# Twenty instead of nineteen score tiles on VectorE in 25 of 64 attention groups, and four follow-up steps moved

## The chip, the cores and the metric

The kernel runs on one core of one Trainium2 chip. The metric is the device time in microseconds of one execution; the number given for a kernel is the median of several executions. A profiled execution comes with a trace of every instruction on the engines: TensorE (PE, its weight loads PEld), VectorE (DVE), ScalarE (ACT), GpSimd (POOL) and SyncE (SP).

## The reference

Two spectral layers and two attention layers alternate, each on a layer norm of the running array x (2048 rows, 512 columns, bf16), each added back to x. The change touches only the attention:

```python
def _B_ref(x, wq, wk, wv, wo):
    B, S, D = x.shape
    H = 32
    Dh = D // H
    q = (x @ wq).reshape(B, S, H, Dh).transpose(0, 2, 1, 3)
    k = x @ wk
    v = x @ wv
    scores = jnp.einsum("bhqd,bkd->bhqk", q, k) * (Dh ** -0.5)
    p = _softmax(scores, axis=-1)
    o = jnp.einsum("bhqk,bkd->bhqd", p, v)
    return o.transpose(0, 2, 1, 3).reshape(B, S, H * Dh) @ wo
...
x = x + _A_ref(_layernorm(x, axis=-1), A_w_r, A_w_i)
x = x + _B_ref(_layernorm(x, axis=-1), B_wq, B_wk, B_wv, B_wo)
x = x + _A_ref(_layernorm(x, axis=-1), A_w_r, A_w_i)
x = x + _B_ref(_layernorm(x, axis=-1), B_wq, B_wk, B_wv, B_wo)
```

There are 32 heads of 16 columns, and one set of keys and values for all of them. So per attention layer there are 32 x 2048 x 2048 exponentials.

## The kernel before

**Groups and tiles.** The kernel has two pairs of (spectral layer, attention layer). `Attention.run` (L560) does one attention layer as 32 groups: 4 blocks of 512 queries times 8 sets of 4 heads. A group has 64 score tiles: 16 blocks of 128 keys times 4 heads; a tile is 128 keys by 512 queries. For every tile TensorE makes the scores in PSUM (`score`, L681), some engine makes the exponential in SBUF, and TensorE multiplies it by the values and a column of ones into the group's sum `pv` (L803).

**Two ways to an exponential.** ScalarE takes 45 of the 64 tiles of a group, 3 and 2 at a time in turn (`OPW`), with its exponential function (`act_step`, L790: `e<-sc`). One such ScalarE instruction is one **step**; a group has 18 steps. VectorE takes the other 19 (`DPOS`, three batches of 6, 7 and 6 tiles). For such a tile it makes one linear map of the scores into 16-bit integers, whose bits read as bf16 are a rough power of two (`dv_pass`, L824: `t_new<-dv`). Three further images of the tile, shifted by fixed amounts, are added with weights to smooth the error: two by VectorE for a whole batch at once (`image_step`, L839: `s_new<-t_new`, 128x3072 for 6 tiles, 128x3584 for 7), one by GpSimd tile by tile (L843: `pool_new<-t_new`). So a VectorE tile costs TensorE one score matmul and four value matmuls, where a ScalarE tile costs one and one.

**Order of a step.** The loop at the end of `run` goes through the steps. In step n it issues, in this order: the scores and the exponential of ScalarE's step (`act_step`), the scores for VectorE's tiles of the step (`dv_score`), what a piece of the step before left for VectorE (`pending`), the turning of a finished group (`evict`, L706), `dv_pass`, what was put off to this step (`todo`), the batch images (`image_step`), what was put off for GpSimd (`todo_pool`), the value matmuls (`pv_step`) and at last a piece. All engines work through their own queue in this order.

Counted from the first step of a group (step 0): batch b is scored in the six steps before step 6b, two tiles in the first of the six where it has seven, else one a step; its two VectorE images are in steps 6b and 6b+3 (`IMG`), and its GpSimd images in steps 6b to 6b+5. In step 3 the group before is turned (L706). Its reciprocals (L707) follow one step later, and GpSimd's scaling (`normalise`, L739, or L717 for the last 8 groups of a layer) three steps after the turn.

**GpSimd's pace.** `pace` makes GpSimd's images and its scaling wait for the VectorE image issued last before them. Nothing makes a VectorE image wait for GpSimd.

**Pieces.** `QSTEP` = 7: in step 7 TensorE projects the queries of the next group (`piece("q")`, L485); VectorE scales them out of PSUM in step 8 (`qcast`, L491) and clears the sign bits of a part of the rows (`qabs`, L495, the "mask of the bound") `QABS` = 1 step after the piece. `OSTEP` = 13: in 12 groups of a layer (9 to 12, 17 to 20, 25 to 28) TensorE projects 128 of the finished outputs (`piece("o")`, L754) in step 13, and VectorE adds the old rows of x in the step after (`residual`, L759). A piece takes one of the two PSUM tiles `dv0`, `dv1`, in which VectorE's scores stand, until VectorE has read it.

In the first layer the new rows get their statistics in groups 13 to 16, 21 to 24 and at the end (L152, L153). In the last layer finished rows are stored.

Of the kernel before, what the change touches and what calls it, by code (L numbers as in the profile page):

```python
# [472 lines left out]
class Attention:  # L473
# [85 lines left out]

    def run(self, row_done, work, psums, final):  # L560
        nc, tc, tabs, x_sb, KT, small = self.nc, self.tc, self.tabs, self.x_sb, self.KT, self.small
# [24 lines left out]
        NG = NQB * HG  # L586
        ops = []
# [13 lines left out]
        for g in range(NG):  # L601
            for b, pos in enumerate(DPOS):
# [4 lines left out]
                steps = [base - BSTEPS + k for k in range(BSTEPS) for _ in range(1 + (len(pos) > BSTEPS and k in TWICE[b]))]  # L607
# [9 lines left out]
        LAG, NBT = 2, max(len(pos) for pos in DPOS)  # L617
        evict_at = {s1[g] + LAG + 1: g for g in range(NG)}
# [22 lines left out]
        for g in range(NG - 1):  # L641
            place(s0[g] + QSTEP, "q", g + 1)
        for qb in range(NQB - 1):
            for i in range(4):
                place(s0[HG * (qb + 1) + 1 + i] + OSTEP, "o", 4 * qb + i)

# [8 lines left out]
        for n in range(NS + LAG + 2):  # L655
            queue += due.get(n, [])
            lst = pv_list[n] = []
            if n in evict_at:
                assert not any(u[0] == evict_at[n] for u in queue)
                continue  # L660
            g = evict_at.get(n + 1)
            rounds = 0 if n in piece_at else ROUNDS[n % 2]
            while queue:
                rnd = full_round(queue if g is None or not any(u[0] == g for u in queue) else [u for u in queue if u[0] == g])
                must = g is not None and any(u[0] == g for u in queue)
                if not must and (rounds <= 0 or len(rnd) < 4 and len(queue) < HOLD):
# [29 lines left out]
        def evict(g):  # L696
# [9 lines left out]
            nc.vector.transpose(out=o.rearrange("p c j -> p (c j)"), in_=ps)  # L706
            later(1, lambda: nc.vector.reciprocal(out=den, in_=o[:, :, DH]))  # L707
            later_pool(3, lambda: normalise(g, o, den))

# [24 lines left out]
        def normalise(g, o, den):  # L734
# [13 lines left out]
            if g % 2:  # L748
                later(3, lambda: turned_back(g))

# [6 lines left out]
        def residual(k, ps):  # L757
            r, t = (k % 4, k // 4)
            nc.vector.tensor_tensor(out=x_sb[:, r, t, :], in0=ps, in1=x_sb[:, r, t, :], op=ALU.add)  # L759
            if t == NQB - 2:  # L760
                n = s0[NG - 3 + r // 2] + (4, 14)[r % 2]
            else:
                n = s0[HG * (t + 1) + 5 + r] + STAT
            later(max(2, n - now[0]), lambda: finish(r, t))
# [41 lines left out]

        held, bank = [None], [0]

# [18 lines left out]
        def image_step(n):  # L827
            if n in d_phase:
                g, b, k, tiles = d_phase[n]
                src, nt = tb[(g, b)].bitcast(I16), len(tiles)  # L830
                if k == 0:
                    pool_new = work.tile([P, NBT, 512], I16, tag="SP", bufs=2)
                    sb[(g, b, 3)] = pool_new
                if k in IMG:
                    i = 1 + IMG.index(k)
                    s_new = work.tile([P, NBT, 512], I16, tag="S", bufs=3)
# [28 lines left out]
        for n in range(NS + LAG + 2):  # L865
            now[0] = n
            act_step(n)
            dv = dv_score(n)
            for fn in pending:
                fn()  # L870
# [53 lines left out]
def full_kernel(ctx, tc, A_x, A_w_r, A_w_i, B_x, B_wq, B_wk, B_wv, B_wo, out, n_pairs=2):  # L924
    nc = tc.nc
# [134 lines left out]
    for pair in range(n_pairs):  # L1060
# [35 lines left out]
        with ExitStack() as ap:  # L1096
            work = ap.enter_context(tc.tile_pool(name=f"workB{pair}", bufs=2, side="right", reuse_waits="tile"))
            psums = [ap.enter_context(tc.tile_pool(name=f"{n}{pair}", bufs=1, space=PSUM, reuse_waits="tile")) for n in ("psc", "psd", "psp")]
            last = att.run(row_done, work, psums, final)
            if final:  # L1100
# [48 lines left out]
```

## Time and profile before

| | |
|---|---|
| median of 3 runs | 1523.18 us (1522.98 to 1523.98) |
| the profiled execution | 1522.62 us, its span 1520.8 us, granted TensorE clock 0.994 |
| steady group without old rows (5 groups, 174.48 to 276.34 us) | 101.86 us, 20.37 us each |
| first attention layer, ScalarE's 579 steps | begin at 106.9 us, the last at 765.0 us |
| second attention layer, ScalarE's 579 steps | begin at 854.5 us, the last at 1511.5 us |

The profile's page gives the busy time of each engine, then the chain of work that ended last, then groups of instructions by line. The windows view gives the busy time of each engine in a stretch, with the count of instructions. In the timeline, instructions of one kind in a row stand as one line with their count; a bracket shows how long the engine sat idle before, and what it waited for. Durations overlap a little: an engine starts the next instruction before the last one has fully ended, so the distance from start to start is the better price of an instruction in a busy queue.

### The profile page before, as it was taken

To read this page: it belongs to the slowest core of one execution; us is meant where nothing else is said; L and a number is where in the kernel's file an instruction comes from. 1 tells how busy PE (TensorE), PEld (TensorE's weight loads), DVE (VectorE), ACT (ScalarE), POOL (GpSimd) and SP (SyncE) were. 2 spreads that over 40 slices of the span, in tenths; PEclk is the share of its full clock that TensorE was granted. 3 is DMA by queue.
4 is the path that set the end of the run, shared out by engine and by line. 5 is a ranking of instruction groups with operands and counts; after the bars stand their busy time and mean duration, and the time that the engine had idled before them with its cause. 6 is when DMAs were issued, how large, how long until landed. Compare 5 with 4: busy or idle time off the path is not lost.

```text
span 1520.8 us, 33089 instructions
## 1 busy us (share of the span) xinstructions
PE 1337.1 (88%) x13186; PEld 427.5 (28%) x13186; DVE 1421.6 (93%) x2267; ACT 1427.3 (94%) x1349; POOL 780.1 (51%) x1310
## 2 busy tenths in 40 slices
PE   5988888899889988999899788889998899889987
PEld 2532222222222222222235222222222222222222
DVE  7888999999999999999989899999999999999996
ACT  4669999999999999999965899999999999999998
POOL 1005555555566555655600155555656555665555
PEclk9999999999999999999999899999999999999999
DMA  8120000100000000100010200000000000010000
GB/s 291 22 56 2 2 1 2 15 2 1 2 16 2 1 1 2 15 2 1 2 47 14 43 1 2 2 1 19 5 2 4 19 5 5 4 19 5 5 5 18
DMA packets 40655, 25.15 MB, mean 17 GB/s; under 512 B 31796, under 2 KB 37940, under 8 KB 40244
## 3 DMA queue, kind: packets, MB, share of 16 engines
q1 hardware_dynamic: 40116, 21.99, 5.8%
q8 instruction: 103, 1.69, 0.5%
q0 software_dynamic: 384, 1.05, 0.2%
q14 instruction: 52, 0.43, 0.1%
HBM read 14.64 MB, written 2.10 MB: 11 GB/s over the span
## 4 chain that ended last, share of the span: by engine, by line
ACT 51%; issue 22%; DVE 15%; PE 7%; POOL 1%; POOLq 0%; DVEq 0%; ACTq 0%
ACT e L790 49%; DVE t_new L824 7%; DVE s_new L839 4%; PE sc L681 1%; PE pv_new L803 1%; DVE st L161 1%; PE new L273 1%; PE new L443 1%; POOL pool_new L843 1%; DVE o L706 1%; PE new L311 0%; PE new L413 0%; DVE x_sb L459 0%; PE dv L681 0%; ACT X_new L188 0%
## 5 line engine op out<-in xcount | busy, mean ns | idle before, releaser
L790 ACT ACTIVATE e<-sc 128x1536 bf16<-128x1536 f32 (+1 forms) x1158 | 1312.7, 1300 | 4.2 <-PE dv L681 2.6
L843 POOL TENSOR_SCALAR pool_new<-t_new 128x512 int16<-128x512 int16 x1204 | 729.5, 629 | 701.9 <-DVE s_new L839 609.3
L824 DVE TENSOR_SCALAR t_new<-dv 128x512 uint16<-128x512 f32 x1204 | 790.1, 678 | 61.7 <-PE dv L681 54.3
L803 PE MATMUL pv_new<-e,vaug 128*32 128x512 bf16 x2892 | 583.3, 386 | 0.0
L681 PE MATMUL sc<-qt,KT 32*128 32x512 bf16 x2892 | 455.1, 384 | 123.4 <-ACT e L790 118.6
L681 PE MATMUL dv<-qt,KT 32*128 32x512 bf16 x1204 | 450.6, 384 | 18.9 <-DVE t_new L824 16.0
L803 PE MATMUL pv_new<-s_new,vaug 128*32 128x512 bf16 x2408 | 426.6, 385 | 1.9 <-DVE s_new L839 1.2
L839 DVE TENSOR_SCALAR s_new<-t_new 128x3584 int16<-128x3584 int16 (+1 forms) x380 | 403.3, 1062 | 0.1
L681 PEld LDWEIGHTS <-KT 32*128 32x128 bf16 x4096 | 157.9, 91 | 563.0 <-issue 559.7
L803 PE MATMUL pv_new<-pool_new,vaug 128*32 128x512 bf16 x1204 | 300.9, 384 | 1.4 <-POOL pool_new L843 1.4
L803 PEld LDWEIGHTS <-vaug 128*32 128x32 bf16 x7708 | 155.2, 94 | 370.4 <-issue 339.0
L803 PE MATMUL pv_new<-t_new,vaug 128*32 128x512 bf16 x1204 | 231.3, 385 | 0.1
L485 PE MATMUL ps<-xz,wq_sb 128*128 128x512 bf16 x248 | 65.2, 385 | 0.9 <-DVE t_new L824 0.8
L273 PE MATMUL new<-tab_F,xz 128*128 128x512 bf16 x192 | 46.5, 389 | 7.4 <-DVE xz L237 7.4
L491 DVE TENSOR_SCALAR qt<-ps,kq 128x512 bf16<-128x512 f32 x62 | 46.0, 742 | 1.2 <-PE ps L485 1.2
L706 DVE STREAM_TRANSPOSE o<-pv_new 128x512 f32<-128x512 f32 x62 | 43.7, 706 | 0.0
L188 ACT ACTIVATE X_new<-x_sb,ln_nb,ln_rstd 128x512 bf16<-128x512 bf16 x43 | 32.8, 804 | 8.0 <-DVE ln_nb L173 5.6
L161 DVE BATCH_NORM_STATS2 st<-x_sb 128x6 f32<-128x512 bf16 x52 | 33.5, 676 | 3.9 <-DMA x_sb<-in_A_x_dram 3.7
L168 ACT ACTIVATE ln_rstd<-ln_mv,ln_eps 128x4 f32<-128x4 f32 (+1 forms) x15 | 4.5, 297 | 30.8 <-DVE ln_mv L165 30.8
L485 PEld LDWEIGHTS <-wq_sb 128*128 128x128 bf16 x256 | 22.1, 97 | 32.2 <-issue 17.1
L739 POOL TENSOR_TENSOR block<-o,den 128x256 bf16<-128x256 f32 x48 | 29.9, 623 | 0.0
L197 ACT CAST x_new<-new 128x1024 bf16<-128x1024 f32 x14 | 14.2, 1012 | 16.4 <-PE new L311 15.1
(125 smaller groups left out, 586.0 us busy)
## 6 DMA issues: line engine op xcount, KB each, us to landing
tab_F<-const_F SPq DMA_DIRECT2D x5, 640.0 KB, 8.6
t_new<-const_IE SPq DMA_DIRECT2D x2, 1024.0 KB
x_sb<-in_A_x_dram SPq DMA_DIRECT2D x3, 512.0 KB, 7.0
rt<-in_A_w_r_dram SPq DMA_DIRECT2D x1, 1028.0 KB, 8.4
rt<-in_A_w_i_dram SPq DMA_DIRECT2D x1, 1028.0 KB, 6.6
t_new<-const_IO SPq DMA_DIRECT2D x2, 512.0 KB
woh<-in_B_wo_dram SPq DMA_DIRECT2D x16, 64.0 KB, 2.4
out_dram<-x_sb SPq DMA_DIRECT2D x8, 128.0 KB, 2.4
```

The source lines that it names most:

```text
L161: self.nc.vector.bn_stats(st, x_t[:, r, :])
L188: engine.activation(out=xn_ap, in_=x_ap, func=ACT.Identity, bias=nb, scale=rs)
L273: self.mm(ps, lhsT=z, rhs=tab, start=start and i == 0, stop=stop and i == len(mms) - 1)
L485: self.nc.tensor.matmul(ps, lhsT=self.aw["wq"][:, c, hg, :], rhs=self.xT[:, 4 * qb:4 * qb + 4, c, :], start=(c == 0), stop=(c == NC - 1))
L491: self.nc.vector.tensor_scalar(out=qt, in0=ps, scalar1=self.kq[:, 1:2], scalar2=None, op0=ALU.mult)
L681: nc.tensor.matmul(dst, lhsT=KT[hs, kc * P:(kc + 1) * P], rhs=QT[g][hs, :], start=True, stop=True)
L706: nc.vector.transpose(out=o.rearrange("p c j -> p (c j)"), in_=ps)
L790: nc.scalar.activation(out=e[:, 0:na, :], in_=sc[:, 0:na, :], func=ACT.Exp, scale=SCALE)
L803: nc.tensor.matmul(pv[g][32 * h:32 * h + 32, :], lhsT=vaug[:, max(j, 0), kc, :], rhs=rhs, start=(first_pv[(g, h)] == u), stop=(last_pv[(g, ...
L824: nc.vector.tensor_scalar(out=tb[(g, b)][:, i, :], in0=dv, scalar1=T_MUL, scalar2=T_ADD, op0=ALU.mult, op1=ALU.add)
L839: image[0] = nc.vector.tensor_scalar(out=s_new[:, lo:nt, :], in0=src[:, lo:nt, :], scalar1=PH_OFF[i], scalar2=None, op0=ALU.add)
L843: pace(nc.gpsimd.tensor_scalar(out=sb[(g, b, 3)][:, i, :], in0=src[:, i, :], scalar1=1.0, scalar2=PH_OFF[3], op0=ALU.mult, op1=ALU.add))
```

## The change

There are now two kinds of groups. Kind N is as before (6, 7, 6 tiles on VectorE). Kind A has batches of 7, 7 and 6, so 20 tiles on VectorE and 44 on ScalarE; one ScalarE instruction of three tiles, in step 16, becomes one of two, and the group still has 18 steps. `PLAN` names the kind of each of the 32 groups: in the first layer groups 1 to 7 are of kind A, in the second groups 1 to 8, 13 to 16, 21 to 24, 29 and 30, in all 25. None of these has old rows to add in it. The rest of the constants move into a table for each layer. In both layers and all groups four follow-ups move: the reciprocals come 2 steps after the turn instead of 1 (`RCP`), GpSimd's scaling 6 instead of 3 steps after it, but for the last 8 groups of a layer (`NRM`), the mask of the bound 3 steps after the piece instead of 1 (`QABS`), and the output projections with their old rows 2 steps later (`OSTEP` 15 instead of 13). `TFIRST` is empty, and the branch for `QABS` of zero isn't taken, so both do nothing.

```diff
-DPOS = ((1, 4, 8, 11, 15, 18), (21, 24, 27, 30, 33, 36, 39), (44, 47, 51, 54, 58, 61))
-SHORT = -1
-TWICE, IMG = ((0,), (0,), (0,)), (0, 3)
+DPOS = ({6: (1, 4, 8, 11, 15, 18), 7: (1, 4, 7, 10, 13, 16, 19)},
+        {7: (21, 24, 27, 30, 33, 36, 39)},
+        {6: (44, 47, 51, 54, 58, 61)})
+KINDS = {"N": (6, 7, 6), "A": (7, 7, 6)}
+LOOPS = (dict(PLAN='NAAAAAAANNNNNNNNNNNNNNNNNNNNNNNN',
+               SHORT=15, IMG=((0, 3), (0, 3), (0, 3)),
...
+               RCP=2, NRM=6, TRN=3, TFIRST=(), ROUNDS=(2, 4), QSTEP=7, QABS=3, OSTEP=15, STAT=14, HOLD=8),
+         dict(PLAN='NAAAAAAAANNNNAAAANNNNAAAANNNNAAN',
...
-ROUNDS, QSTEP, OSTEP, STAT, HOLD, QABS = (2, 4), 7, 13, 14, 8, 1
...
+        positions = lambda g: [DPOS[b][k] for b, k in enumerate(KINDS[C["PLAN"][g]])]
+        ops, begun = [], {}
         stream = [(g, p // 4, p % 4) for g in range(NG) for p in range(64)
-                  if not any(p in pos for pos in DPOS[g == 0:])]
+                  if not any(p in pos for pos in positions(g)[g == 0:])]
         while stream:
-            w = OPW[len(ops) % 2] - (len(ops) % 18 == SHORT)
+            g = stream[0][0]
+            n = len(ops) - begun.setdefault(g, len(ops))
+            tiles = sum(KINDS[C["PLAN"][g]])
+            w = OPW[len(ops) % 2] - (tiles == 20 and n == C["SHORT"] + (begun[g] + C["SHORT"]) % 2)
...
-            later(1, lambda: nc.vector.reciprocal(out=den, in_=o[:, :, DH]))
-            later_pool(3, lambda: normalise(g, o, den))
+            later(C["RCP"], lambda: nc.vector.reciprocal(out=den, in_=o[:, :, DH]))
+            later_pool(3 if g >= NG - HG else C["NRM"], lambda: normalise(g, o, den))
...
-                later(QABS, lambda: qabs(QT[k]))
+                if C["QABS"]:
+                    later(C["QABS"], lambda: qabs(QT[k]))
+                else:
+                    unsigned.append(lambda: qabs(QT[k]))
```

More of the change, by code (lines that the diff above doesn't have):

```diff
@@ L558, in ready, with run @@
         nc.vector.tensor_scalar(out=qt, in0=qt, scalar1=kq[:, 1:2], scalar2=None, op0=ALU.mult)
-    def run(self, row_done, work, psums, final):
+    def run(self, row_done, work, psums, final, pair):
+        C = LOOPS[pair]
         nc, tc, tabs, x_sb, KT, small = self.nc, self.tc, self.tabs, self.x_sb, self.KT, self.small
@@ L601, in run @@
         for g in range(NG):
-            for b, pos in enumerate(DPOS):
+            for b, pos in enumerate(positions(g)):
                 if g == 0 and b == 0:
@@ L606, in run @@
                 tiles = [(p // 4, p % 4) for p in pos]
-                steps = [base - BSTEPS + k for k in range(BSTEPS) for _ in range(1 + (len(pos) > BSTEPS and k in TWICE[b]))]
+                steps = [base - BSTEPS + k for k in C["DK"][b, len(pos)]]
                 clash = lambda pm: sum(any(u[2] == tiles[i][1] for u in ops[n]) for n, i in zip(steps, pm)) + \
@@ L665, in run @@
                 must = g is not None and any(u[0] == g for u in queue)
-                if not must and (rounds <= 0 or len(rnd) < 4 and len(queue) < HOLD):
+                if not must and (rounds <= 0 or len(rnd) < 4 and len(queue) < C["HOLD"]):
                     break
@@ L748, in normalise @@
             if g % 2:
-                later(3, lambda: turned_back(g))
+                later(C["TRN"], lambda: turned_back(g))
         def outproj(k, ps):
@@ L868, in run @@
             dv = dv_score(n)
+            if C["TFIRST"] and (n in evict_at and C["TFIRST"][1] or pending and C["TFIRST"][0]):
+                dv_pass(n, dv)
+                dv = []
             for fn in pending:
@@ L1098, in full_kernel @@
             psums = [ap.enter_context(tc.tile_pool(name=f"{n}{pair}", bufs=1, space=PSUM, reuse_waits="tile")) for n in ("psc", "psd", "psp")]
-            last = att.run(row_done, work, psums, final)
+            last = att.run(row_done, work, psums, final, pair)
             if final:
```

24 lines of the change are left out of this document (15 added, 9 removed).

## The prediction

> **What bounds the kernel now.** I read the page first, for the engines' busy times and the chain that ended last.
>
> ```profile
> span 1520.8 us, 33089 instructions
> PE 1337.1 (88%) x13186; PEld 427.5 (28%) x13186; DVE 1421.6 (93%) x2267; ACT 1427.3 (94%) x1349; POOL 780.1 (51%) x1310
> ACT 51%; issue 22%; DVE 15%; PE 7%; POOL 1%; POOLq 0%; DVEq 0%; ACTq 0%
> ```
>
> ScalarE and VectorE are both nearly full, so the average doesn't say which of them sets the pace. The stretches do: five steady groups without old rows; one group with them; the most loaded group of the first layer; the two groups before the last of the second.
>
> ```profile
> core 0: us, PE busy (x) PEld busy (x) DVE busy (x) ACT busy (x) POOL busy (x), PEclk, DMA share, GB/s
> 174.48:276.34 101.86, 89.02 (x948) 26.70 (x945) 96.35 (x147) 101.86 (x91) 59.67 (x101) 1.00 0.01 2
> 296.72:317.11 20.39, 19.02 (x196) 5.37 (x193) 19.75 (x32) 20.39 (x19) 11.92 (x21) 1.00 0.01 2
> 726.75:748.20 21.45, 18.67 (x192) 5.45 (x189) 21.12 (x35) 21.10 (x20) 14.05 (x25) 1.00 0.01 2
> 1453.30:1494.00 40.70, 35.56 (x381) 10.61 (x378) 39.07 (x60) 40.70 (x37) 25.69 (x43) 1.00 0.02 8
> ```
>
> In the steady stretch ScalarE is busy for all of 101.86 us: it sets 20.37 us a group. VectorE needs 96.35 / 5 = 19.27 and has 1.10 to spare; with old rows 0.64. In the loaded group the order is turned: VectorE 21.12 of 21.45, and ScalarE waits. So a group takes about the longer of the two sums, and when VectorE is the longer, some 0.33 us of it is still idle. I take the groups of the same stretch by form next.
>
> ```profile
> L790 ACT ACTIVATE e<-sc 128x1536 bf16<-128x1536 f32 x46 | 70.6, 1535 | 0.0
> L824 DVE TENSOR_SCALAR t_new<-dv 128x512 uint16<-128x512 f32 x96 | 63.2, 679 | 5.5 <-PE dv L681 4.7
> L790 ACT ACTIVATE e<-sc 128x1024 bf16<-128x1024 f32 x45 | 50.0, 1111 | 0.0
> L681 PE MATMUL sc<-qt,KT 32*128 32x512 bf16 x227 | 35.6, 381 | 11.6 <-ACT e L790 11.6
> L803 PE MATMUL pv_new<-pool_new,vaug 128*32 128x512 bf16 x95 | 23.2, 384 | 0.0
> L839 DVE TENSOR_SCALAR s_new<-t_new 128x3072 int16<-128x3072 int16 x20 | 19.0, 948 | 0.0
> L839 DVE TENSOR_SCALAR s_new<-t_new 128x3584 int16<-128x3584 int16 x10 | 12.8, 1284 | 0.0
> ```
>
> ScalarE never sits idle; VectorE's idle time ends with PE's scores, which wait for ScalarE. The odd number is the last: a seventh tile lengthens an image from 948 to 1284 ns, 336 for one sixth more work. The timeline of one steady group shows why.
>
> ```profile
> 255.95 0.71 DVE L706 STREAM_TRANSPOSE o<-pv_new 128x512 f32<-128x512 f32 x1
> 256.58 0.65 DVE L824 TENSOR_SCALAR t_new<-dv 128x512 uint16<-128x512 f32 x1
> ...
> 258.62 0.24 DVE L707 RECIPROCAL den<-o 128x16 f32<-128x16 f32 x1
> 258.77 1.38 DVE L824 TENSOR_SCALAR t_new<-dv 128x512 uint16<-128x512 f32 x2
> 260.07 1.08 DVE L839 TENSOR_SCALAR s_new<-t_new 128x3584 int16<-128x3584 int16 x1
> 261.07 0.68 DVE L824 TENSOR_SCALAR t_new<-dv 128x512 uint16<-128x512 f32 x1
> 261.67 0.74 DVE L491 TENSOR_SCALAR qt<-ps,kq 128x512 bf16<-128x512 f32 x1
> 262.33 0.68 DVE L824 TENSOR_SCALAR t_new<-dv 128x512 uint16<-128x512 f32 x1
> 262.92 0.35 DVE L495 TENSOR_SCALAR qt<-qt,tab_QAND 128x512 int16<-128x512 int16 x1
> 263.19 0.68 DVE L824 TENSOR_SCALAR t_new<-dv 128x512 uint16<-128x512 f32 x1
> 263.79 1.48 DVE L839 TENSOR_SCALAR s_new<-t_new 128x3584 int16<-128x3584 int16 x1
> 265.20 1.90 DVE L824 TENSOR_SCALAR t_new<-dv 128x512 uint16<-128x512 f32 x3
> 267.01 0.95 DVE L839 TENSOR_SCALAR s_new<-t_new 128x3072 int16<-128x3072 int16 x1
> 267.88 1.28 DVE L824 TENSOR_SCALAR t_new<-dv 128x512 uint16<-128x512 f32 x2
> 269.37 0.69 DVE L824 TENSOR_SCALAR t_new<-dv 128x512 uint16<-128x512 f32 x1 [0.21 <-PE dv L681]
> ...
> 273.05 1.29 DVE L824 TENSOR_SCALAR t_new<-dv 128x512 uint16<-128x512 f32 x2 [0.73 <-PE dv L681]
> ```
> ```profile
> 261.33 1.20 POOL L843 TENSOR_SCALAR pool_new<-t_new 128x512 int16<-128x512 int16 x2 [1.37 <-PE ps L485]
> 262.50 0.62 POOL L739 TENSOR_TENSOR block<-o,den 128x256 bf16<-128x256 f32 x1
> 263.09 1.25 POOL L843 TENSOR_SCALAR pool_new<-t_new 128x512 int16<-128x512 int16 x2
> 265.36 1.79 POOL L843 TENSOR_SCALAR pool_new<-t_new 128x512 int16<-128x512 int16 x3 [1.03 <-DVE s_new L839]
> ```
>
> The batch of seven has its first image (step 6, at 260.07) in 1.08 us and its second (step 9, at 263.79) in 1.48, though they are alike. GpSimd was then still at work until 263.09 + 1.25 = 264.34, so 0.55 of the second image ran beside it and cost 0.40. GpSimd was late because its scaling ("block") stood between its images.
>
> **The change part by part.** From start to start in a full VectorE queue: a tile (267.01 - 265.20) / 3 = 0.60; an image of six 0.87 (267.01 to 267.88); of seven 1.00 alone, 1.41 beside GpSimd; the query scaling 0.66, the mask 0.27, the turn 0.63, the reciprocal 0.15.
>
> *ScalarE in an A group* loses one tile of one instruction: 1535 - 1111 = 424 ns. Its pace becomes 20.37 - 0.42 = 19.95.
>
> *VectorE in an A group* gets one tile (0.60) and two images longer by 1.00 - 0.87 = 0.13: 0.86 more. That is inside the 1.10 only if nothing else is lost. The scaling's move out of the steps between the images of the seven-tile batch takes away the 0.40, but the images of batch 0 now run beside more GpSimd work. I go through the group, VectorE never waiting, time 0 at the image of step 0. GpSimd starts 0.18 after an image has ended (260.07 + 1.08 to 261.33) and takes 0.60 an operation.
>
> - Step 0's image 1.00, two tiles, the turn, a tile: the image of step 3 starts at 3.43. GpSimd's four tiles end at 1.26 + 2.40 = 3.66: 0.23 beside it, at 0.40 / 0.55 some 0.17.
> - Then 1.17, three tiles and the reciprocal: step 6 at 6.55. GpSimd's three tiles end at 4.86 + 1.79 = 6.65: 0.10 beside, 0.07.
> - Then 1.07, three tiles and the query scaling; the mask is gone from here: step 9 at 10.08. GpSimd's four tiles, without the scaling, end at 7.88 + 2.40 = 10.28: 0.20 beside, 0.15.
> - Then 1.15, four tiles (two of them the new batch's in step 12) and the mask: step 12 at 13.90. GpSimd's three tiles and now the scaling end at 11.49 + 2.40 = 13.89: none.
> - Then 0.87 and three tiles, 0.87 and four tiles: the next step 0 at 19.84, of which 0.39 is time beside GpSimd.
>
> The Trainium skill (SBUF — State Buffer, "Who interferes with whom") states that a VectorE instruction in a two-port mode and GpSimd exclude each other, and that the later one blocks until the first has finished. By that the overlaps would count in full, 0.53 instead of 0.39, and an A group would come out 0.14 longer on VectorE (at most 3.2 us over 23 groups, so up to 1519.7 where the row gives 1516.5); the one overlap quoted above cost 0.40 of 0.55, less than the rule says.
>
> The same walk over a group of before gives 19.84 - 0.86 - 0.39 + 0.41 = 19.00, where the row has 19.27: the walk may be 0.27 short. So VectorE in an A group needs 19.84 to 20.11, ScalarE 19.95, and the group takes between 19.95 and 20.11 + 0.33 = 20.44, if the idle time of the loaded group comes on top. I take 20.08, near the upper sum without that idle time, since an A group's load is even over the steps (images at 0, 3.43, 6.55, 10.08, 13.90, 16.57, against 3.3 each at ScalarE's pace), while the loaded group has extra work in a few. That is 0.29 less a group.
>
> *The last two* (groups 29, 30 of the second layer) keep the scaling 3 steps after the turn, so the 0.41 stays: 39.07 / 2 + 0.86 = 20.40 of VectorE against 20.35 before: nothing to win, up to 0.4 to lose each. I put them at 0.
>
> *TensorE* makes three matmuls more in an A group, from 3 x 0.244 = 0.73 (23.2 / 95) to 3 x 0.384 = 1.15, or less where four heads run side by side; it waits 11.6 / 5 = 2.32 a group for ScalarE, and even after the 0.42 there is room. Three short ScalarE steps now follow each other (15, 16, 17); if TensorE were late there the group would lose some tenths, which the upper end holds.
>
> *The moves in N groups* cost nothing that I can see. The contact of scaling and image goes from step 9 to step 12: after step 9's image, 1.00 + 0.60 x 3 + 0.27 = 3.07 to the next, GpSimd done at 3.66, 0.59 beside it. VectorE's sum stays, and 1.10 (0.64 with old rows) covers it; without cover it would be 0.4 a group. The mask in step 10 must be done before TensorE's scores of the next group in step 12; it lies two VectorE tiles ahead, so a wait there is 0 to 0.15, within the 0.27. The scaling of each eighth group issues four transposing DMAs on SyncE's queue, now three steps (3.4 us) later; the projection that reads them comes over a group later, and itself two steps later. GpSimd queues three tiles of images ahead of the scaling, and nothing else waits for that. The added old rows move from step 14 to 16, where VectorE has its idle time (0.73 at 273.05); gain or loss is about 0.02 (20.39 against 20.37) in each of 24 groups, put at 0. The reciprocal moves one step and its reader three.
>
> The sum: 23 x 0.29 = 6.7 us. From the profiled execution's 1522.62 that gives 1515.9; the median of before lies 0.56 above that execution, so **1516.5 us**.
>
> **The rivals.** *ScalarE's pace is reached in full:* VectorE keeps up. 25 x 0.42 = 10.5, so 1512.7. For it speaks that the walk's 19.84 is below 19.95; against, that no slack is left.
>
> *VectorE takes over, with idle time:* 20.3 to 20.44 a group, a gain of 1.6 to a loss of 1.6: 1521.6 to 1524.8, no change. For it speaks the loaded group's 0.33.
>
> *GpSimd's lateness spreads:* an A group has four seven-tile images. If each catches GpSimd at work as step 9's did, VectorE needs 19.45 + 4 x 0.41 = 21.09, and 23 x 0.72 = 16.6 make it 1539.8, slower. It decides from 0.65 us of contact cost in a cycle (20.37 - 19.45 - 0.27); my walk has 0.39. Against it: a contact makes the next image later, which gives GpSimd time, so contacts don't add up freely.
>
> *The move doesn't do what it says:* if GpSimd's scaling still ran before step 9's image, VectorE would be at 20.25 to 20.5: no change again.
>
> **How the numbers follow.** This kernel's measurement tells 0.2%, 3.05 us, from no change: faster is below 1520.1, slower above 1526.2. My forecast has 0.50, the full ScalarE pace 0.21; both are faster: 0.71. Idle VectorE and the unmoved scaling have 0.17 as no change. The spread of contacts, at part or full price, has 0.12 as slower. The range runs from a microsecond under ScalarE's full pace, for the few uneven groups that may even out, 1511.5, to the upper end of no slack, 1524.8; it leaves out the slow rival and a little below, some 0.15.
>
> **What would show it.** In A groups, ScalarE's 44 tiles with VectorE at 20.0 busy and about 0.1 idle; seven-tile images at 1.08 to 1.25 and none at 1.48 in the first layer's groups 1 to 7; the 1.4 us images in N groups now six-tile ones at step 12; N groups unchanged at 20.37 to 20.39. Wrong would be: A groups at 20.4 or more with ScalarE waiting for scores; or scores of ScalarE's waiting for VectorE's PSUM tile, which would mean that the order of TensorE's queue, not the sum, decides.

## The result, and the profile after

The changed kernel takes 1519.76 us (median of 18 runs, 1518.31 to 1522.24) where the kernel before takes 1523.15 on the same chip (18 runs): a ratio of 0.9975, 95% interval 0.9968 to 0.9981. It is faster by 0.25%, 3.4 us, half of the 6.7 of the forecast. The profiled execution takes 1520.78 us, 1.84 less than the one of before. The page of the changed kernel, its span, busy times and the chain that ended last by engine:

```profile
span 1519.0 us, 33248 instructions
PE 1358.4 (89%) x13220; PEld 423.3 (28%) x13261; DVE 1436.7 (95%) x2292; ACT 1420.6 (94%) x1349; POOL 794.1 (52%) x1335
DVE 41%; ACT 25%; PE 18%; issue 11%; POOL 1%; DVEq 0%; POOLq 0%; ACTq 0%
```

VectorE gains 15.1 us of work and ScalarE loses 6.7. The chain has turned over: ScalarE's share falls from 51% to 25%, TensorE's rises from 7% to 18%. The windows of the changed kernel, with the columns of the forecast's: three A groups; an N group with old rows; groups 12 and 28 of the second layer, which stand ahead of an A group; then the beginning of each attention layer.

```profile
core 0: us, PE busy (x) PEld busy (x) DVE busy (x) ACT busy (x) POOL busy (x), PEclk, DMA share, GB/s
175.42:235.88 60.46, 56.14 (x576) 14.96 (x576) 59.34 (x91) 60.25 (x55) 37.48 (x64) 1.00 0.01 1
316.95:337.32 20.37, 18.69 (x193) 5.52 (x193) 19.74 (x31) 20.37 (x19) 11.90 (x21) 1.00 0.00 1
1104.03:1125.34 21.31, 19.39 (x193) 5.38 (x194) 20.33 (x33) 21.01 (x19) 11.91 (x21) 1.00 0.01 2
1430.53:1451.80 21.27, 19.40 (x193) 5.43 (x194) 20.69 (x34) 20.86 (x19) 11.91 (x21) 1.00 0.00 1
104.00:134.00 30.00, 23.82 (x225) 7.55 (x225) 22.60 (x37) 27.10 (x32) 7.76 (x13) 0.87 0.00 1
855.00:881.00 26.00, 22.32 (x185) 5.72 (x184) 20.30 (x30) 24.88 (x23) 8.65 (x15) 0.78 0.01 2
```

An A group takes 60.46 / 3 = 20.15 us, not 20.08. VectorE is busy for 59.34 / 3 = 19.78 of it and ScalarE for 20.08: neither is full. The N group is as forecast. Groups 12 and 28 take 21.3 us; both engines wait in them.

From the start of one turn (L706 before, L719 after) to the next, all groups of both profiled executions compare so:

| stretch | before to after |
|---|---|
| the 23 A groups of the forecast | 4.98 us shorter (0.22 in most; 0.36 in the last of each run of them, 20.37 to 20.02; nothing in group 23 of the second layer; group 1 of the second layer 0.21 longer) |
| groups 29 and 30 of the second layer | 0.34 shorter |
| groups 12, 20 and 28 of the second layer | 0.90, 0.20 and 0.68 longer |
| all other groups but each layer's last, summed | 0.48 shorter (two uneven groups of the first layer 0.39 each, less small losses) |
| the first layer's last turn | 0.30 later after the one before |
| up to the first turn; from the first layer's last turn to the second's first | 1.44 and 0.44 longer |

Sum: 4.98 + 0.34 - 1.78 + 0.48 - 0.30 - 1.88 = 1.84, the difference of the two executions. In the last row's stretches TensorE's granted clock is lower: 0.97 and 0.96 before, 0.95 and 0.94 after. Most of the 1.88 is probably that; no run tells it apart. Two windows of the kernel before, to be set against the last two above (0.87 and 0.78):

```profile
104.00:134.00 30.00, 23.08 (x227) 7.32 (x225) 22.93 (x37) 28.41 (x33) 9.74 (x16) 0.89 0.00 1
855.00:881.00 26.00, 21.56 (x184) 6.12 (x184) 20.08 (x30) 24.96 (x23) 9.18 (x15) 0.81 0.01 2
```

**Inside an A group.** VectorE's timeline in one A group of the changed kernel, and GpSimd's scaling in it:

```profile
216.95 1.17 DVE L855 TENSOR_SCALAR s_new<-t_new 128x3584 int16<-128x3584 int16 x1
...
219.94 1.07 DVE L855 TENSOR_SCALAR s_new<-t_new 128x3584 int16<-128x3584 int16 x1
220.93 0.68 DVE L837 TENSOR_SCALAR t_new<-dv 128x512 uint16<-128x512 f32 x1
221.53 0.73 DVE L499 TENSOR_SCALAR qt<-ps,kq 128x512 bf16<-128x512 f32 x1
222.19 1.47 DVE L837 TENSOR_SCALAR t_new<-dv 128x512 uint16<-128x512 f32 x2
223.58 1.08 DVE L855 TENSOR_SCALAR s_new<-t_new 128x3584 int16<-128x3584 int16 x1
...
226.31 1.29 DVE L837 TENSOR_SCALAR t_new<-dv 128x512 uint16<-128x512 f32 x2 [0.19 <-PE dv L694]
227.51 0.95 DVE L855 TENSOR_SCALAR s_new<-t_new 128x3072 int16<-128x3072 int16 x1
...
230.18 1.04 DVE L855 TENSOR_SCALAR s_new<-t_new 128x3072 int16<-128x3072 int16 x1
...
233.69 1.08 DVE L855 TENSOR_SCALAR s_new<-t_new 128x3584 int16<-128x3584 int16 x1
```
```profile
225.33 0.67 POOL L752 TENSOR_TENSOR block<-o,den 128x256 bf16<-128x256 f32 x1
```

The image of step 9 (223.58) is down from 1.48 to 1.08, and the scaling now runs behind it. So the move does what it says. Yet VectorE, to which the forecast gave about 0.1 us of idle time, waits 0.19 for TensorE's scores here alone. The chain of waits of the same kernel, each piece with start, duration, engine and work, over one whole period:

```profile
200.86 0.61 DVE t_new L837
201.47 0.04 issue
201.51 0.37 PE dv L694
201.88 0.55 PE pv_new L816 x8
...
202.75 0.76 PE pv_new L816 x12
...
205.84 0.23 PE dv L694
...
206.16 1.29 DVE t_new L837 x2
...
221.01 0.61 DVE t_new L837
221.62 0.04 issue
221.66 0.37 PE dv L694
```

ScalarE isn't in this period. From 201.47 the chain runs on TensorE (steps 8 to 12) for 4.69 us, until VectorE gets its next pair of tiles at 206.16. From there it stays on VectorE for 15.46, up to the end of the tile of step 7 at 221.62, where TensorE may start its scores of step 8. 4.69 + 15.46 = 20.15, the group. TensorE has to wait for that tile because the query projection holds the other of the two PSUM tiles: VectorE reads it out (L499) only at 221.53, right behind the tile. Ahead of the projection VectorE and TensorE take turns on two tiles, here on one. The kernel before already had this wait, at the same place of a steady group:

```profile
221.06 0.37 PE L681 MATMUL dv<-qt,KT 32*128 32x512 bf16 x1 [0.23 <-DVE t_new L824]
```

### The profile page after: what moved, and what is told of

The parts are those of the page before. It is cut to its first block, busy times and chain, and to the rows that moved or that the text cites. A ratio compares the mean times of both kernels' runs of the same rounds, so it can differ in the third digit from the quotient of the medians.

```text
span 1519.0 us, 33248 instructions
## 1 busy us (share of the span) xinstructions
PE 1358.4 (89%) x13220; PEld 423.3 (28%) x13261; DVE 1436.7 (95%) x2292; ACT 1420.6 (94%) x1349; POOL 794.1 (52%) x1335
## 4 chain that ended last, share of the span: by engine, by line
DVE 41%; ACT 25%; PE 18%; issue 11%; POOL 1%; DVEq 0%; POOLq 0%; ACTq 0%
ACT e L803 24%; DVE t_new L837 23%; DVE s_new L855 12%; PE pv_new L816 6%; PE sc L694 4%; PE dv L694 2%; DVE o L719 2%; DVE st L169 1%; PE new L281 1%; PE ps L767 1%; POOL pool_new L859 1%; PE new L451 1%; DVE den L720 0%; DVE x_sb L467 0%; PE new L319 0%
## 5 line engine op out<-in xcount | busy, mean ns | idle before, releaser
L803 ACT ACTIVATE e<-sc 128x1024 bf16<-128x1024 f32 (+1 forms) x1158 | 1306.1, 1298 | 7.7 <-PE dv L694 3.6
L859 POOL TENSOR_SCALAR pool_new<-t_new 128x512 int16<-128x512 int16 x1229 | 741.4, 625 | 686.4 <-DVE s_new L855 587.4
L837 DVE TENSOR_SCALAR t_new<-dv 128x512 uint16<-128x512 f32 x1229 | 803.0, 679 | 42.9 <-PE dv L694 32.3
L694 PE MATMUL dv<-qt,KT 32*128 32x512 bf16 x1229 | 463.4, 383 | 20.3 <-DVE t_new L837 17.3
L816 PE MATMUL pv_new<-s_new,vaug 128*32 128x512 bf16 x2458 | 404.7, 384 | 0.7
L694 PEld LDWEIGHTS <-KT 32*128 32x128 bf16 x4096 | 152.1, 91 | 546.0 <-issue 538.4
L816 PE MATMUL pv_new<-pool_new,vaug 128*32 128x512 bf16 x1229 | 254.6, 385 | 1.5 <-POOL pool_new L859 1.4
L499 DVE TENSOR_SCALAR qt<-ps,kq 128x512 bf16<-128x512 f32 x62 | 45.8, 739 | 1.2 <-PE ps L493 1.2
L719 DVE STREAM_TRANSPOSE o<-pv_new 128x512 f32<-128x512 f32 x62 | 43.8, 706 | 0.2 <-PE pv_new L816 0.2
L205 ACT CAST x_new<-new 128x1024 bf16<-128x1024 f32 x14 | 14.2, 1012 | 16.4 <-PE new L319 15.1
```

The lines of the kernel that those rows point to most:

```text
L499: self.nc.vector.tensor_scalar(out=qt, in0=ps, scalar1=self.kq[:, 1:2], scalar2=None, op0=ALU.mult)
L694: nc.tensor.matmul(dst, lhsT=KT[hs, kc * P:(kc + 1) * P], rhs=QT[g][hs, :], start=True, stop=True)
L803: nc.scalar.activation(out=e[:, 0:na, :], in_=sc[:, 0:na, :], func=ACT.Exp, scale=SCALE)
L816: nc.tensor.matmul(pv[g][32 * h:32 * h + 32, :], lhsT=vaug[:, max(j, 0), kc, :], rhs=rhs, start=(first_pv[(g, h)] == u), stop=(last_pv[(g, ...
L837: nc.vector.tensor_scalar(out=tb[(g, b)][:, i, :], in0=dv, scalar1=T_MUL, scalar2=T_ADD, op0=ALU.mult, op1=ALU.add)
L859: pace(nc.gpsimd.tensor_scalar(out=sb[(g, b, 3)][:, i, :], in0=src[:, i, :], scalar1=1.0, scalar2=PH_OFF[3], op0=ALU.mult, op1=ALU.add))
```

## The experiments

Each kernel is the changed one with the edit shown; ratios are to the kernel before on the same chip, with 95% intervals.

### Which half of the change pays: moves alone, tiles alone

```diff
-LOOPS = (dict(PLAN='NAAAAAAANNNNNNNNNNNNNNNNNNNNNNNN',
+LOOPS = (dict(PLAN='NNNNNNNNNNNNNNNNNNNNNNNNNNNNNNNN',
...
-         dict(PLAN='NAAAAAAAANNNNAAAANNNNAAAANNNNAAN',
+         dict(PLAN='NNNNNNNNNNNNNNNNNNNNNNNNNNNNNNNN',
```

> All 64 groups of kind N, the four moves kept. My theory, that the moves by themselves cost and win next to nothing because ScalarE sets the pace of N groups: the steady N group stays at 20.37 us, and the whole at 1522 to 1523.5 us, ratio to before 0.9990 to 1.0002 (the uneven groups of the first layer, such as 20.76 and 20.77, may go to 20.38). The rival, that the moves carry the change's gain: 1520 us or less, ratio 0.998 or less.

1521.79 us (11 runs), ratio 0.9992 (0.9984 to 1.0001): the moves alone give next to nothing, as the theory had it. The two uneven groups of the first layer stay uneven (20.72 each).

The second kernel keeps the A groups and takes back the four moves, in both layers:

```diff
-               RCP=2, NRM=6, TRN=3, TFIRST=(), ROUNDS=(2, 4), QSTEP=7, QABS=3, OSTEP=15, STAT=14, HOLD=8),
+               RCP=1, NRM=3, TRN=3, TFIRST=(), ROUNDS=(2, 4), QSTEP=7, QABS=1, OSTEP=13, STAT=14, HOLD=8),
```

> The 25 A groups kept, the reciprocals, the scaling, the mask and the output projections back at their old steps (1, 3, 1 and 13). My theory, that the moves are what makes room on VectorE: a seven-tile image of step 9 keeps its 1.48 us, VectorE needs 20.2 or more in an A group, an A group takes 20.3 to 20.6 us, and the whole is 1522 to 1527 us, ratio 0.9992 to 1.0025. The rival, that an A group is not set by VectorE's sum: A groups at 20.15 as with the moves, ratio 0.9975 or below.

1522.39 us (11 runs), ratio 0.9990 (0.9981 to 0.9998). Three of its A groups, and its image of step 9:

```profile
176.28:236.75 60.47, 55.97 (x578) 15.22 (x576) 60.17 (x91) 60.26 (x56) 37.43 (x64) 1.00 0.01 1
```
```profile
205.21 1.48 DVE L855 TENSOR_SCALAR s_new<-t_new 128x3584 int16<-128x3584 int16 x1
```

The theory missed, and of the rival the group's time came, but not the ratio. The contact with GpSimd is back at 1.48, VectorE's work is 0.28 a group higher (60.17 / 3 = 20.06), and the group takes 20.16 us all the same. So VectorE's sum of 19.78 isn't what sets the changed kernel's group: step 9's image lies beside TensorE's part of the loop (203.18 to 207.98 here), where VectorE has time to spare. This kernel is slower than the changed one mostly by its clock (0.9874 in the mean of its runs against 0.9901): its five runs at 0.986 take 1522.8 in the mean, the changed kernel's five at that clock (the control below included) 1522.2. The other 0.6 fits its second layer, which is 0.55 us longer from its first turn to that of group 30.

### The moved old rows against the new batch

```diff
-         dict(PLAN='NAAAAAAAANNNNAAAANNNNAAAANNNNAAN',
+         dict(PLAN='NAAAAAAAANNNNNAAANNNNNAAANNNNNAN',
```

> As changed, but groups 13, 21 and 29 of the second layer of kind N, so that no seven-tile batch is scored in the steps in which old rows are added (22 A groups). My theory: groups 12, 20 and 28, which rose to 21.31, 20.96 and 21.27 us, come back to 20.4 to 20.6, some 2.2 us won, against 0.4 to 0.6 lost on the three groups that are N again: 1.6 to 1.8 us less than the changed kernel, ratio to before 0.9960 to 0.9968. The rival, that these groups are long for another reason: they stay, and the whole is 0.4 to 0.6 us longer than the changed kernel, ratio 0.9978.

1518.39 us (6 runs), ratio 0.9969 (0.9957 to 0.9980), with three A groups fewer. Groups 12, 20 and 28 take 20.73, 20.39 and 20.55 us instead of 21.31, 20.96 and 21.27. The first of them:

```profile
1105.03:1125.76 20.73, 18.70 (x192) 5.56 (x193) 19.87 (x32) 20.63 (x19) 11.92 (x21) 1.00 0.01 2
```

Group 13 (and 21 and 29) of kind A has seven tiles in its first batch, which are scored in steps 12 to 17 of the group ahead. In that group the output projection holds a PSUM tile in step 15, and the old rows come in step 16. The loss sits where both meet. From the second layer's first turn to that of group 30 this plan takes 2.06 us less; 0.45 of that is its group 1, which ran at a better clock (0.97 against 0.94), so 1.6 is the plan's, as the theory had it. It wins 1.87 in the three groups and loses 0.64 in groups 13, 21 and 29, which are N again.

Group 23 wins as well: it takes 20.15 here and 20.38 in the changed kernel. There GpSimd issues a store of finished rows (L1112) just as VectorE's image of step 15 begins, and the image takes 1.41 instead of 1.04:

```profile
1343.13 1.41 DVE L855 TENSOR_SCALAR s_new<-t_new 128x3072 int16<-128x3072 int16 x1
```
```profile
1343.00 0.58 POOL L1112 DMA_DIRECT2D out_dram<-x_sb  x1
```

This image lies on VectorE's part of the loop, and the group is 0.23 longer than its neighbours. So a contact with GpSimd has a price here, and had none beside TensorE's part.

The next kernel undoes the old rows' move alone, everywhere:

```diff
-               RCP=2, NRM=6, TRN=3, TFIRST=(), ROUNDS=(2, 4), QSTEP=7, QABS=3, OSTEP=15, STAT=14, HOLD=8),
+               RCP=2, NRM=6, TRN=3, TFIRST=(), ROUNDS=(2, 4), QSTEP=7, QABS=3, OSTEP=13, STAT=14, HOLD=8),
```

> As changed, but the output projections at step 13 and the old rows at step 14 again. The theory that it is the load of the six steps from 12 to 17 that counts, wherever in them the old rows lie: groups 12, 20 and 28 of the second layer stay within 0.3 us of 21.31, 20.96 and 21.27, and the whole within 0.8 us of the changed kernel, ratio 0.9973 to 0.9983. The rival, that the place of the old rows counts (step 16 close before the two tiles of the next group's step 0): these three groups fall by 0.5 us or more each, ratio 0.9965 or less.

1523.54 us (11 runs), ratio 1.0003 (0.9994 to 1.0012): all of the gain is gone, which was not expected.

```profile
318.71:339.28 20.57, 18.69 (x195) 5.35 (x193) 19.87 (x32) 20.50 (x19) 11.91 (x21) 1.00 0.00 1
```

An N group with old rows takes 20.57 us here, against 20.37 with all four moves and 20.41 with none. Groups 12, 20 and 28 come out at 21.54, 21.19 and 21.50, within 0.3 of the changed kernel's, as the theory had it, and about as with no move at all (21.54, 21.19, 21.30). So step 14 is no better a place for the old rows, and the three groups are long without any move. With the moves and no A group they take 20.38, 20.41 and 20.53 (first kernel above). So it is the A group behind them that makes them long. For the N groups the moves hang together: next to the other three, the old rows have to be late too. Which of the three asks for it wasn't told apart.

### What holds an A group at 20.15

A control first: the changed kernel as it is, built again.

> The changed kernel as it is, beside the next three on one chip, and for the granted clock of its runs. Both theories: 1519 to 1521 us, ratio to before 0.9970 to 0.9982. If the granted clock explains the spread of its runs, the runs with the lower clock are the slower ones, by some 0.5 us for each 0.001.

1521.07 us (10 runs), ratio 0.9983 (0.9974 to 0.9993). The intervals of the two measurements of the changed kernel overlap; this one, just outside what was expected, has a mean clock of 0.9871, the first 0.9901. Its runs at a lower clock are the slower ones: 1522.2 at 0.986 (4 runs), 1520.3 at 0.987 (5 runs), 1518.15 at 0.992 (one).

Then the TensorE part of the loop is changed. In every other step four rounds of value matmuls are allowed; with three, three matmuls of an A group move from step 5 to step 11:

```diff
-               ... ROUNDS=(2, 4), ...
+               ... ROUNDS=(2, 3), ...
```

> As changed, but at most three rounds of value matmuls in an odd step instead of four: in A groups alone, three matmuls move from step 5 to step 11, and nothing else. My theory: an A group is held at 20.15 us not by VectorE (it is 20.16 with 20.07 busy in the run without the moves) but by TensorE, which goes into the query projection of step 7 one round (0.22 us) late, so that ScalarE waits 0.46 us there instead of 0.25. Then A groups fall to 19.93 to 20.0, and the whole by 3 to 5 us against the changed kernel on this chip. The rival, VectorE with its idle time: A groups stay at 20.1 to 20.2, and the whole within 1 us.

1521.35 us (10 runs), ratio 0.9985 (0.9976 to 0.9994).

```profile
154.56:215.08 60.52, 55.97 (x576) 15.27 (x576) 59.15 (x92) 60.31 (x55) 37.50 (x64) 1.00 0.01 1
```

60.52 / 3 = 20.17: no gain, as the rival had it. In this kernel's chain TensorE's part is 4.85 (200.79 to 205.64) and VectorE's 15.32 (205.64 to 220.96). The one got 0.16 longer, the other 0.14 shorter. So VectorE's part isn't all work: two tiles near the group's end take 1.27 in the changed kernel's chain (211.07 to 212.34), with a wait for scores, and 1.13 here (210.55 to 211.68).

Next the projection moves behind the tight place, from step 7 to 9, with the mask one step after it:

```diff
-               ... QSTEP=7, QABS=3, ...
+               ... QSTEP=9, QABS=1, ...
```

> As changed, but the query projection two steps later (step 9) with its mask one step after it, at its old distance. Theory, that the 0.25 us that ScalarE loses in each group comes from the projection so soon after the step of the turn, in which TensorE does no value matmuls: N groups fall from 20.37 to 20.1 to 20.25, A groups to 19.95 to 20.1, the whole by 5 to 10 us against the changed kernel. The rival, that the mask then comes too late for the scores of the next group's first batch in step 12, and TensorE waits there: groups stay or get longer, the whole within 1 us or up to 10 us longer.

1544.53 us (4 runs), ratio 1.0141 (1.0125 to 1.0158), worse than any expectation. An A group, and an N group with old rows:

```profile
174.33:194.48 20.15, 18.40 (x192) 5.12 (x192) 20.05 (x31) 20.09 (x19) 13.28 (x22) 1.00 0.01 2
316.95:337.96 21.01, 18.58 (x193) 5.58 (x193) 19.84 (x31) 20.45 (x19) 11.99 (x21) 1.00 0.01 1
```

The A group stays at 20.15, but not by the same loop. Its chain from 174 to 195 us has no piece of TensorE any more: it stays on VectorE, whose work is 0.27 higher, in the main because the mask now runs beside GpSimd (0.61 instead of 0.35 us). Here VectorE's own queue is the limit, and that it comes to the same 20.15 is chance. The last A group of each run, with an N group behind it, falls from 20.02 to 19.86.

The loss is in the N groups, with old rows or without: 0.64 in most of them. VectorE has hardly more work there (19.84 against 19.74) and waits. The chain of the group shown names the wait. TensorE's scores for VectorE at 326.22 wait for the query scaling, which stands in VectorE's queue behind the tile (323.42) and the image of step 9, 1.39 us long. So it is again a projection that holds one of the two PSUM tiles, now behind a whole image.

The head order of the first batch is spread next, so that two tiles meet in step 13 of the group ahead instead of step 12, and a tile of the third batch moves to another head:

```diff
-        {6: (44, 47, 51, 54, 58, 61)})
+        {6: (44, 47, 51, 54, 56, 61)})
...
-   (0, 7): (0, 0, 1, 2, 3, 4, 5)
+   (0, 7): (0, 1, 1, 2, 3, 4, 5)
```

> As changed, but with the score matmuls of an A group's steps 11 and 12 on different heads: the two tiles of the seven-tile batch 0 in step 13 (an odd step, two ScalarE tiles) instead of 12, and one tile of batch 2 at another position (56 for 58, in all groups). My theory now: the loop that holds an A group at 20.15 runs over VectorE from step 12 to 7 and over TensorE from step 8 to 12, where TensorE never waits and two score matmuls of one head queue behind each other, 0.22 us each. Without them the loop is 0.43 shorter, but the image of step 12 then meets GpSimd's scaling again (0.2 to 0.4): A groups at 19.95 to 20.1, none over 20.15, N groups as they are, the whole 1 to 4 us under the changed kernel. The rival, VectorE's sum with its idle time: A groups at 20.1 to 20.2 and the whole within 1 us.

1525.64 us (11 runs), ratio 1.0012 (1.0003 to 1.0021). The A group, and a piece of the chain of waits:

```profile
177.20:197.56 20.36, 18.56 (x192) 5.16 (x192) 19.84 (x31) 20.08 (x19) 12.49 (x22) 1.00 0.01 2
```
```profile
204.73 0.97 PE pv_new L816 x15
205.70 0.33 PE sc L694 x3
...
206.13 1.46 ACT e L803
```

It missed: the edit regrouped the value matmuls, and 15 of them instead of 12 now stand in step 9 (0.97 instead of 0.76); behind them the chain goes through ScalarE. But it shows that another order, with VectorE's work 0.06 higher and ScalarE's the same, can take the whole gain of an A group. On top of it, GpSimd's scaling comes later:

```diff
-               RCP=2, NRM=6, ...
+               RCP=2, NRM=12, ...
```

> As the last, and GpSimd's scaling 12 steps after the turn instead of 6 (in step 15, between images of six tiles), so that neither the image of step 9 nor that of step 12 meets it. My theory: the loop is then shorter than ScalarE's work, so A groups come to ScalarE's pace, 19.93 to 20.0, and the whole to 3 to 5 us under the changed kernel. The rival: another wait takes its place at 20.05 to 20.2, and the whole is within 1.5 us of the changed kernel.

1524.00 us (11 runs), ratio 1.0005 (0.9996 to 1.0014). A groups stay at 20.36 with VectorE at 19.78, longer than either expectation. Groups 16 and 24 of the first layer, 20.85 and 20.80 with the spread head order alone, fall to 20.42. That, with the plan clear of old rows:

```diff
-         dict(PLAN='NAAAAAAAANNNNAAAANNNNAAAANNNNAAN',
+         dict(PLAN='NAAAAAAAANNNNNAAANNNNNAAANNNNNAN',
```

> As the last, and groups 13, 21 and 29 of the second layer of kind N. My theory: about 1.5 to 2 us under the last, ratio to before 0.994 to 0.996; the rival as before: 1.5 to 2 us under the changed kernel, 0.9965 to 0.997.

1522.30 us (11 runs), ratio 0.9993 (0.9984 to 1.0002), short of both expectations: the head order costs more than the rest brings.

The last kernel takes one round of value matmuls out of the loop, from step 9 to 13 in A groups, on top of the plan clear of old rows:

```diff
             rounds = 0 if n in piece_at else C["ROUNDS"][n % 2]
+            here = max((q for q in range(NG) if s0[q] <= n), default=0)
+            if C["PLAN"][here] == "A" and 9 <= n - s0[here] <= 12:
+                rounds = min(rounds, 2)
```

> The kernel without A groups at old rows (groups 13, 21 and 29 of kind N, as in the third run), and in A groups at most two rounds of value matmuls in the steps 9 to 12: the third round of step 9 goes to step 13, nothing else changes. My theory: an A group is held by a loop of VectorE from step 12 to the tile of step 7 (15.46 us) and TensorE from there to the scores of step 12 (4.62 us); one round less on TensorE's part takes 0.21 off it, so A groups go from 20.15 to 19.94 to 20.0, ScalarE's pace, and the whole 3 to 4.5 us under the third run's kernel at the same granted clock. The rival, that VectorE's sum with an unavoidable idle time holds the group: A groups stay at 20.12 to 20.2, the whole is that of the third run, ratio 0.9965 to 0.9972.

1518.05 us (6 runs), ratio 0.9966 (0.9954 to 0.9978), the lowest median here, though its interval overlaps the changed kernel's and is nearly that of the plan alone (0.9969). The 3 to 4.5 us of the theory didn't come. Three steady A groups and the last A group ahead of an N; then pieces of the chain in a steady one:

```profile
174.29:234.71 60.42, 55.58 (x576) 15.30 (x576) 59.32 (x91) 60.23 (x55) 37.48 (x64) 1.00 0.01 1
254.85:274.69 19.84, 18.10 (x191) 5.05 (x191) 19.43 (x31) 19.84 (x19) 12.49 (x22) 1.00 0.01 2
```
```profile
207.29 1.46 ACT e L806
...
208.79 0.39 PE sc L697 x2
```

Where the next group has one tile less, the group falls from 20.02 to 19.84, and there ScalarE shows no idle time. A steady group falls only from 20.15 to 20.14. The loop of steps 8 to 12 has become shorter, and another of nearly the same length, through ScalarE's step 14 and TensorE's steps 16 to 18, ends last instead. Which matmul of that second loop would have to go was not tried. So no edit made a steady A group shorter than 20.14: what is shown is that in the changed kernel neither engine's sum holds it, and by the chain which loop ends last. That the group would reach ScalarE's pace without these loops is not shown.

### The clock at the beginning of a layer

Groups 1 to 3 of both layers become N, to see whether the denser A groups bring the clock down:

```diff
-LOOPS = (dict(PLAN='NAAAAAAANNNNNNNNNNNNNNNNNNNNNNNN',
+LOOPS = (dict(PLAN='NNNNAAAANNNNNNNNNNNNNNNNNNNNNNNN',
...
-         dict(PLAN='NAAAAAAAANNNNAAAANNNNAAAANNNNAAN',
+         dict(PLAN='NNNNAAAAANNNNAAAANNNNAAAANNNNAAN',
```

> As changed, but groups 1 to 3 of each layer of kind N (19 A groups), to see the stretches at half TensorE clock at the begin of each attention layer. Theory, that the denser work of A groups right after the begin brings more of these stretches: the mean granted clock rises to that of before (0.991), group 1 is 20.4 and never 21.4, and the whole is within 0.7 us of the changed kernel, for 6 x 0.22 = 1.3 us of gain is given up and about as much won back. The rival, that the stretches have nothing to do with the kind of group: the clock as with the changed kernel, and the whole 1.0 to 1.6 us longer.

1521.14 us (10 runs), ratio 0.9984 (0.9974 to 0.9993), mean clock 0.9882. The clock didn't come back to the 0.9907 of the kernel before. The whole is the control's, though six A groups fewer give up 1.3 us: neither expectation fits in full. Group 1, now of kind N, ran in the profiled execution at 0.90 and took 21.40:

```profile
135.71:157.11 21.40, 19.43 (x192) 5.29 (x190) 19.37 (x29) 20.27 (x19) 11.38 (x20) 0.90 0.01 2
```

So the clock falls there without A groups too.

## Why the prediction was half right

**The direction held: one tile less takes ScalarE off the path.** Its pace was read wrongly. I took "busy for all of 101.86 us" to mean that it sets 20.37 us a group. In the trace its steps start 0.90 us after a step of two tiles and 1.33 after one of three wherever they don't wait: 9 x 0.904 + 9 x 1.33 = 20.11 us in an N group and 10 x 0.904 + 8 x 1.33 = 19.68 in an A group, not 19.95. The rest are waits that don't show as idle time, because a step that starts at its own pace overlaps the one before it. The chain of the kernel before has two, behind the query projection: 1.39 us after a step of three tiles, then 1.09 after one of two.

```profile
220.10 0.78 ACT e L790
...
221.01 1.34 ACT e L790
...
222.40 1.05 ACT e L790
...
223.49 0.82 ACT e L790
```

**The walk over VectorE held up to step 15.** From the image of step 0 (213.54, one period ahead of 233.69) the next images start at 3.41, 6.40, 10.04, 13.97 and 16.64; forecast were 3.43, 6.55, 10.08, 13.90 and 16.57. From there to the next step 0 it had 3.27, and it took 3.51. Contacts came out smaller: the walk had 0.39 in a cycle, the rows some 0.2. The contact image of step 3 took 1.09 from start to start, where the walk had 1.17.

**The failed reason: "even after the 0.42 there is room".** TensorE has room in its sum, but not between VectorE's tile of step 7 and its pair of step 12. I took a group to last about as long as its longest sum. It lasts as long as the longest loop through the engines, and in a steady A group of the changed kernel that loop goes over TensorE and VectorE. So the 0.29 a group became 0.22, and 6.7 us became 4.98 (0.45 of it lost in the second layer's group 1 at a lower clock, 0.23 in group 23). That 20.15 lies so near to my 20.08 is luck: I had it from VectorE's sum, which came out at 19.78 and is no bound. Where I called the upper end's 0.33 of idle time possible, the idle time came, 0.37, for this other reason. In the kernel with the tiles alone the contact at step 9 costs VectorE 0.28 and the group nothing: the half of the change that I priced most closely has no price in an A group.

**The missing term: the group ahead of an A group.** "The moves in N groups cost nothing that I can see" was right for most N groups, as the moves alone show. What has no term in the sum is the seventh tile of an A group's first batch: it is scored in the last six steps of the group ahead, and that group paid nothing in my sum. In groups 12, 20 and 28 these steps also hold the old rows. I wrote that those go "where VectorE has its idle time (0.73 at 273.05)". But with old rows there are only 0.64 to spare, and the tile takes 0.60 of them before anything waits. The three groups lost 0.90 + 0.20 + 0.68 = 1.78 us, and the plan that clears them wins 1.87 back in them. They are no shorter without the moves (21.54, 21.19, 21.30). In the chain of the changed kernel's group 12 the output projection stands on the path, between VectorE's tiles and TensorE's scores: the same shape as the query projection's loop. The same chain has a piece of 0.40 on VectorE at 1107.36 that is named issue. By the timeline it is in part the reciprocal (1107.29, 0.24 us), and then 0.21 us of idle time for which no releaser is named. It stays with the clear plan, whose group 12 still takes 20.73; its cause is open.

**What I left at 0 and was about 0:** most N groups with old rows and an N group behind them (20.37 to 20.38 against 20.40 to 20.41); groups 29 and 30 (0.34 won). The two uneven groups of the first layer (20.76 and 20.77 before) evened out to 20.37 and 20.38, which the range had for its lower end. Groups 16 and 24, with GpSimd's statistics, lost 0.15 each, most likely to the moved scaling: with the spread head order, putting it six steps later still took them from 20.85 and 20.80 to 20.42.

**The rivals.** ScalarE's full pace was not reached. VectorE with idle time described a group rightly (0.37 of it idle), but not its time (20.3 to 20.44) or its cause. GpSimd's lateness did not spread. The move did what it says. The last paragraph's sign, scores "waiting for VectorE's PSUM tile, which would mean that the order of TensorE's queue, not the sum, decides", is close to what came: it is the scores for VectorE that wait for the tile, and ScalarE's stand behind them in TensorE's queue. I had given it no chance and no price.

**The sum.** 6.7 becomes 4.98 + 0.34 - 1.78 + 0.48 = 4.02 over the groups; less 0.30 at the first layer's end it is 3.72, and the medians have 3.4. The other tenths are probably the clock. The profiled pair shows only 1.84; its two executions differ in the clock (0.994 and 0.990).

## What to carry to other kernels

When no engine is full, look for the loop: cut the chain of waits to one period and add up its pieces by engine; only work on that chain has a price, and shortening it helps only as far as the next loop. An engine whose instructions overlap can wait without showing idle time: compare the distances from start to start. A piece that holds one of two buffers makes the other a single one for as long as it stands, so producer and consumer then take turns. When work is moved into an engine's idle time, look at what each kind of neighbouring group puts into the same steps, not only at the group that it was measured in.

## What the runs showed of the hardware

**TensorE's clock at the beginning of a layer differs from run to run.** In the two windows of each kernel shown above, with TensorE busy for 77 to 86% of the time, the granted clock is 0.78 to 0.89, in steady groups 1.00. The same kernel comes out at different times by it: on one chip the kernel before takes 1525.3 us at a mean clock of 0.988 (3 runs), 1522.9 at 0.992 (12 runs) and 1521.95 at 0.994 (one run), about 0.55 us for each 0.001. The changed kernel takes 1520.27 at 0.987 (5 runs of its control) and 1518.77 at 0.992 (4 runs, another measurement), about 0.3 for each 0.001. The mean was 0.9871 and 0.9901 in two measurements of the changed kernel, 0.9907 to 0.9912 in those of the kernel before, 0.9915 with N groups alone, so that some of what one kernel seems to lose to another is this. The Trainium skill (TensorE: Matmul & The Clock Gate, Part 1) describes a gate to half speed that is decided in free-running windows of 3.4 us and varies from run to run; the spread agrees with it, and in the two profiled executions the stretches at half clock at the beginnings of the attention layers last about 3.4, 6.8 or 10.2 us. What the runs don't show is why it falls in these stretches, where TensorE hardly rests.

**Contact of VectorE's images with GpSimd costs less than the shared time.** In the tiles-alone kernel the image of step 9 and GpSimd overlap by 0.53 us and it takes 0.40 more; where they overlap by 0.22, 0.09 more. By the full block that the forecast cited from the Trainium skill (SBUF — State Buffer, "Who interferes with whom") it would be 0.53 and 0.22; in both, 0.13 less was paid.
